# Gated block with a sliding, dilated attention: low halves of weights written by accumulating transfers, and tiles moved to multiples of 256 bytes

## The chip, the cores and the metric

The kernel runs on one core of one Trainium2 chip. The metric is device time in microseconds (us) of one execution, the median of several. Before the change it is 787.69 us, the median of 3 runs (787.12 to 788.05).

A core has a matrix engine (TensorE, PE in the profile; its weight loads stand apart as PEld), three engines that work element by element (VectorE or DVE, ScalarE or ACT, GpSimd or POOL), SyncE (SP), which issues transfers, and 16 DMA engines that move data between the main memory and SBUF, the core's memory of 128 partitions. A matmul has a stationary operand, which a weight load brings into the array, and a moving operand, which is streamed through it; both come from SBUF. Sums come out in PSUM.

## The reference

One block of 2048 tokens, 640 wide, in float32. With `xn` the layer norm of `x`:

```
qkv  = xn @ wqkv                      # 640 x 1920, 32 heads of 20
s    = attention(q, k, v) @ wo        # each token sees itself and 7 others, 2 apart
g    = silu(((xn @ w_gate) * (xn @ w_up)) @ w_down)    # inner width 1536
out  = x + s * g
```

## The kernel before, in words

**Two halves for every operand.** TensorE reads its operands as `float32r`, a rounded form of float32. To keep the precision, each operand is split in two: `hi`, the value rounded to `float32r`, and `lo`, the rest. A product is then three: hi by hi, hi by lo, lo by hi (`ALL3`, line 88; `mm3`, line 90, runs through the inner dimension once for each pair). Lines 83 to 86 make the halves of a weight: ScalarE copies `raw` to `hi`, which rounds, and then the engine that the caller names subtracts; for weights that is GpSimd, in all calls of this part.

**What runs on TensorE.** `qkv` (line 286) makes q, k and v for one of 12 units (6 groups of heads by 2 halves of the tokens): per tile of 128 tokens 15 matmuls, with the tokens `xT` stationary and `wqh` or `wql` moving, 300 columns (groups of 5 heads) or 360 (groups of 6). `gate_up` (line 387) makes one piece (f, ch), 128 columns of gate and of up for 512 tokens: 15 matmuls of 512 columns for each, with the weights `wf` stationary and `xT` moving. f runs from 0 to 11 and ch from 0 to 3. `out_proj` multiplies by `wo` (line 477) and `product` by `w_down` (line 596, with 7 products in place of 8); both have 320 columns.

**The order is written out by hand**, one engine's queue after the other's in program order. After a start with f = 0 and 1, units and pieces alternate: a unit of 8 tiles, then 3 or 4 pieces. In piece (f, 0) SyncE loads the raw weights of f + 1 (`load_wf`); in piece (f, 1), between gate and up, they are split (`split_wf`, line 123). The next group's q, k, v weights are loaded in the third tile of an odd unit (`load_wq`) and split at its end (`split_wq`, line 109), since `wqh` and `wql` have one buffer each, which this unit reads. VectorE works on the attention of earlier units in small steps between the products `hs` of gate and up (`advance`, line 371).

**Where tiles lie.** Tiles stand in a partition one behind the other, in the order in which their tags first appear, each rounded up to 32 bytes. In the built program the tags `t`, `wraw`, `xc` (which holds `xT` and later most of `w_down`), `o` and `ident` start 128 bytes past a multiple of 256; `wqh` starts 32 past one and `wql` 64; `q`, `kv`, `wf`, `mask`, `sel`, `gs`, `hs`, `ot`, `lg` and `e` start 96 past one. The rows that TensorE reads in `wf`, `xc` and the later weights are 512, 2048 or 1280 bytes apart, all multiples of 256, so every row stands as its tile does. The rows of `wqh` and `wql` are 1200 or 1440 bytes long and follow each other directly, so that each of the five stands differently: of `wqh` (300 columns) at 32, 208, 128, 48 and 224 past a multiple of 256, of `wql` at 64, 240, 160, 80 and 0.

Of the kernel before, what the change touches and what calls it, by code (L numbers as in the profile page):

```python
# [12 lines left out]
F32R = mybir.dt.float32r  # L13
AF = mybir.ActivationFunctionType
ALU = mybir.AluOpType
# [4 lines left out]
P = 128  # L20
# [6 lines left out]
KD, KF = D // P, F // P  # L27
# [23 lines left out]
def kernel(  # L51
# [11 lines left out]
    nc = tc.nc  # L63
# [11 lines left out]
    def st(shape, tag, bufs, dt=F32):  # L75
        cnt[0] += 1
        return sb.tile(shape, dt, tag=tag, bufs=bufs, name=f"{tag}_{cnt[0]}")

    def pt(shape, tag, bufs):
        cnt[0] += 1  # L80
        return ps.tile(shape, F32, tag=tag, bufs=bufs, name=f"{tag}_{cnt[0]}")

    def split(eng, raw, hi, lo):

        nc.scalar.activation(hi, raw, AF.Copy)  # L85
        eng.tensor_sub(lo, raw, hi.bitcast(F32))  # L86

    ALL3 = ((0, 0), (0, 1), (1, 0))

    def mm3(acc, pairs, parts=ALL3, first=True, last=True):  # L90

        pairs = list(pairs)
        runs = [(a[i], b[j]) for i, j in parts for a, b in pairs]
        for n, (a, b) in enumerate(runs):
            nc.tensor.matmul(acc, a, b, start=first and n == 0, stop=last and n == len(runs) - 1)  # L95


    wq_raw, wq = {}, {}
# [10 lines left out]
    def split_wq(g, eng, ks=(0, KD)):  # L109
        c3 = 3 * GROUPS[g] * DH  # L110
        if g not in wq:
            wq[g] = st([P, KD, c3], "wqh", 1, F32R), st([P, KD, c3], "wql", 1, F32R)
        for k0, k1, t in wq_raw[g]:
            if ks[0] <= k0 < ks[1]:
                split(eng, t, wq[g][0][:, k0:k1], wq[g][1][:, k0:k1])

    wf_raw, wf = {}, {}

# [3 lines left out]

    def split_wf(f, eng, cuts=(0, KD)):
        hi, lo = st([P, KD, 2, P], "wf", 4, F32R), st([P, KD, 2, P], "wf", 4, F32R)
        for k0, k1 in zip(cuts, cuts[1:]):
            split(eng, wf_raw[f][:, k0:k1], hi[:, k0:k1], lo[:, k0:k1])
        wf[f] = hi, lo


# [2 lines left out]
    def load_x(s, n, t, cuts=(0, D)):  # L132
        j = tile_column(s)
        for c0, c1 in zip(cuts, cuts[1:]):
            nc.sync.dma_start(t[:, :, c0:c1], (xbv if s < NE else xv)[:, j:j + DIL * (n - 1) + 1:DIL, c0:c1])  # L135
        for i in range(n):
            xt[s + i] = t[:, i, :]

    xa, xe = st([P, 3, D], "t", 2), st([P, 3, D], "t", 2)
    load_x(0, 1, xa[:, 0:1], (0, HALF, D))  # L140
    load_x(1, 1, xa[:, 1:2])
# [110 lines left out]
    def trans_odd(s):  # L252
# [7 lines left out]
        low_parts()  # L260
        halves.append(lambda: nc.vector.tensor_sub(lo, y, hi.bitcast(F32)))


    UN = [(g, r) for g in range(len(GROUPS)) for r in range(DIL)]
    q_t, kv_t, kv_buf, kv_zero = {}, {}, {}, {}
# [17 lines left out]

    ALL_RUNS = [(a, b, k) for a, b in ALL3 for k in range(KD)]

# [141 lines left out]
    def gate_up_first(f, ch):  # L427

        pp = [pt([P, CH], "g", 2), pt([P, CH], "u", 2)]
        for parts, first in ((ALL3[:2], True), (ALL3[2:], False)):  # L430
            for n in range(2):
# [6 lines left out]
    def load_wo(ks):  # L438
        t = st([P, 2, D], "wraw", 3)
        for n, k in enumerate(ks):  # L440
            nc.sync.dma_start(t[:, n, :], wo[:, k, :])
            wo_raw[k] = t[:, n, :]
        return t
# [192 lines left out]
    norm(0, 1)  # L636
    mv1 = moments(1, 1)
    split_wq(0, nc.gpsimd, (0, 2))
    trans(0)
    split_wq(0, nc.gpsimd, (2, 3))  # L640
    norm(1, 1, mv1)
    split_wq(0, nc.gpsimd, (3, KD))
    load_x(12, 1, xa[:, 0:1])
    begin_unit(0, False)
# [4 lines left out]
    moments(3, 1, mv2[:, 1:2])  # L649
    load_x(13, 1, xa[:, 1:2])  # L650
    split_wf(0, nc.gpsimd, range(KD + 1))
    norm(2, 2, mv2)
    qkv(0, 1)
    split_wf(1, nc.gpsimd, range(KD + 1))
    zero_front(0)
    part0 = gate_up_first(0, 0)
# [52 lines left out]
    gate_up(1, 2)  # L709
    gate_up(0, 3)  # L710
    split_wf(2, nc.gpsimd)
    gate_up(1, 3)

# [35 lines left out]
    for ch in range(NCH):  # L749
        gate_up(f0, ch)  # L750
        if ch == 0:
# [3 lines left out]
            t = load_wo((4,))  # L755
# [112 lines left out]
```

## Time and profile before

| | |
|---|---|
| median of 3 runs | 787.69 us (787.12 to 788.05) |
| the profiled execution | span 786.0 us from the first to the last instruction |
| mean granted TensorE clock | 0.999 |
| TensorE busy | 778.0 us, 4454 matmuls |
| weight loads busy | 708.9 us, beside the matmuls |
| VectorE, ScalarE, GpSimd busy | 659.3, 234.2, 147.9 us |
| read from and written to main memory | 54.53 MB, 28.31 MB |
| DMA engines, mean busy share of queue 1 | 38.2% |

The profile was taken in an execution of its own, so its span, 786.0 us, stands 1.7 us below the median of the timed runs. A row of a group has the line, the engine, the operation, the output and the inputs by tile name, the shape, the count, then the busy time and the mean of one in ns, and last the idle time of the engine in front of them with what ended it. In the chain of waits each row has a start, a duration and what the time was spent on; it is followed back from the last instruction. A row of the timeline has a start, the time to the end of the last of its instructions, the engine, and the instructions. A row of a table by stage has the stretch and its length, then for each engine the busy time and the count of instructions, the granted clock, the DMA share and GB/s.

### The profile page before, as it was taken

How to read it: one execution, taken by the hardware profiler on the slowest of the kernel's cores; microseconds unless marked ns; L12 is line 12 of the kernel's file. 1: busy time of each engine (PE TensorE's matmuls, PEld its weight loads, DVE VectorE, ACT ScalarE, POOL GpSimd, SP SyncE). 2: the span in 40 equal slices, each digit the busy share in tenths (PEclk: the TensorE clock that was granted, in tenths of full speed). 3: DMA queues.
4: the chain of work that ended last, by engine and by line, in shares of the span. 5: the costliest groups of instructions: out<-in, count | busy, mean ns of one | idle time of the engine just before them, and what ended most of it. 6: DMA issues, size and time to landing. Idle time of an engine off the chain costs nothing.

```text
span 786.0 us, 11222 instructions
## 1 busy us (share of the span) xinstructions
PE 778.0 (99%) x4454; PEld 708.9 (90%) x4454; DVE 659.3 (84%) x660; ACT 234.2 (30%) x536; POOL 147.9 (19%) x110
## 2 busy tenths in 40 slices
PE   8999999999999999999999999999999999999997
PEld 6889898888898898899898989888899999999997
DVE  6889899999999979996999999992177667777775
ACT  5334211121112111311221202012366564444442
POOL 5301211022013200410231000112467600000000
PEclk9999999999999999999999999999999999999999
DMA  8172122141132321404033131332797574555534
GB/s 321 67 230 75 42 61 72 48 123 48 50 83 89 95 71 61 117 28 112 28 105 86 58 86 58 107 103 66 160 274 209 170 270 131 206 200 188 182 101 135
DMA packets 81661, 92.68 MB, mean 118 GB/s; under 512 B 23032, under 2 KB 63304, under 8 KB 81480
## 3 DMA queue, kind: packets, MB, share of 16 engines
q1 hardware_dynamic: 81608, 91.96, 38.2%
q8 instruction: 35, 0.57, 0.3%
q14 instruction: 18, 0.15, 0.1%
HBM read 54.53 MB, written 28.31 MB: 105 GB/s over the span
## 4 chain that ended last, share of the span: by engine, by line
PE 97%; DMA 2%; ACT 1%; DVE 0%; SPq 0%; POOL 0%; issue 0%
PE q L295 26%; PE u L95 21%; PE g L95 21%; PE q L606 11%; PE q L95 9%; PE u L606 5%; PE g L606 3%; DMA wraw<-in_wgu 1%; DMA wraw<-in_wqkv 1%; PE q L229 0%; ACT wf L85 0%; SPq L135 0%; ACT wqh L85 0%; ACT xc L230 0%; POOL wql L86 0%; PE q L249 0%
## 5 line engine op out<-in xcount | busy, mean ns | idle before, releaser
L95 PE MATMUL u<-xc,wf 128*128 128x512 f32 (+1 forms) x735 | 176.2, 390 | 0.0
L95 PE MATMUL g<-xc,wf 128*128 128x512 f32 (+1 forms) x735 | 176.1, 390 | 0.0
L95 PEld LDWEIGHTS u<-xc,wf 128*128 128x128 f32 x735 | 135.7, 187 | 32.2
L95 PEld LDWEIGHTS g<-xc,wf 128*128 128x128 f32 x735 | 135.3, 187 | 31.0
L295 PE MATMUL q<-wqh,xc 128*128 128x300 f32 (+1 forms) x960 | 159.8, 309 | 2.1 <-DVE xc L231 1.2
L295 PEld LDWEIGHTS q<-wqh,xc 128*128 128x128 f32 x960 | 146.0, 188 | 4.3 <-DVE xc L231 1.5
L329 DVE TENSOR_TENSOR t<-q,kv 128x1600 f32<-128x1600 f32 (+1 forms) x48 | 97.9, 2040 | 10.1 <-DMA kv<-kv 10.1
L350 DVE TENSOR_TENSOR t<-e,kv 128x1600 f32<-128x1600 f32 (+1 forms) x48 | 97.5, 2051 | 1.1
L86 POOL TENSOR_TENSOR wf<-wraw,wf 128x256 fp32r<-128x256 f32 (+2 forms) x22 | 48.8, 2232 | 248.1 <-ACT wf L85 248.1
L332 DVE TENSOR_REDUCE lg<-t 128x80 f32<-128x1600 f32 (+1 forms) x48 | 92.6, 1930 | 1.2
L397 ACT ACTIVATE gs<-g 128x512 f32<-128x512 f32 x48 | 28.7, 598 | 205.9 <-PE g L95 197.2
L295 PE MATMUL q<-wql,xc 128*128 128x300 f32 (+1 forms) x480 | 86.3, 309 | 0.0
L358 DVE TENSOR_TENSOR t<-t,t 128x1600 f32<-128x1600 f32 (+1 forms) x36 | 80.2, 2228 | 1.1
L295 PEld LDWEIGHTS q<-wql,xc 128*128 128x128 f32 x480 | 74.4, 188 | 0.0
L297 ACT ACTIVATE kv<-q 128x200 f32<-128x200 f32 (+1 forms) x96 | 33.4, 348 | 129.4 <-PE q L295 129.4
L606 PE MATMUL q<-xc,wf 128*128 128x320 f32 x432 | 67.3, 309 | 0.0
L606 PEld LDWEIGHTS q<-xc,wf 128*128 128x128 f32 x432 | 64.3, 188 | 0.0
L86 POOL TENSOR_TENSOR wql<-wraw,wqh 128x300 fp32r<-128x300 f32 (+4 forms) x15 | 34.0, 2292 | 142.7 <-ACT wqh L85 142.7
L95 PE MATMUL q<-wf,wf 128*128 128x320 f32 x156 | 35.7, 310 | 0.0
L408 DVE TENSOR_TENSOR hs<-u,gs 128x512 f32<-128x512 f32 x39 | 26.6, 683 | 0.6 <-issue 0.6
L95 PEld LDWEIGHTS q<-wf,wf 128*128 128x128 f32 x156 | 26.1, 188 | 0.0
L86 DVE TENSOR_TENSOR wf<-ot,wf 128x640 fp32r<-128x640 f32 x13 | 15.5, 1190 | 11.9 <-ACT wf L85 11.9
(161 smaller groups left out, 888.9 us busy)
## 6 DMA issues: line engine op xcount, KB each, us to landing
h_scr<-hs SPq DMA_DIRECT2D x48, 256.0 KB, 2.3
wraw<-in_wgu SPq DMA_DIRECT2D x12, 640.0 KB, 4.9
t<-h_scr SPq DMA_DIRECT2D x8, 768.0 KB, 7.8
hs<-s_scr SPq DMA_DIRECT2D x16, 320.0 KB, 4.0
gs<-in_x SPq DMA_DIRECT2D x16, 320.0 KB, 4.4
wraw<-h_scr SPq DMA_DIRECT2D x12, 384.0 KB, 5.9
out<-q SPq DMA_DIRECT2D x14, 320.0 KB, 3.7
wraw<-in_wd SPq DMA_DIRECT2D x12, 320.0 KB, 4.8
```

The source lines that it names most:

```text
L86: eng.tensor_sub(lo, raw, hi.bitcast(F32))
L95: nc.tensor.matmul(acc, a, b, start=first and n == 0, stop=last and n == len(runs) - 1)
L295: nc.tensor.matmul(p, xT[(r * NE + i) // TPC][a][:, k, t0:t0 + P], wq[g][b][:, k], start=n == 0, stop=n == len(runs) - 1, skip_group_check ...
L297: nc.scalar.activation(kv_t[u][:, :, W - 1 + i, :], p[:, c:].rearrange("p (a c) -> p a c", a=2), AF.Copy)
L329: nc.vector.tensor_mul(t, q.rearrange("p i c -> p (i c)").unsqueeze(1).to_broadcast([P, 2, NE * c]), places(0, j))
L332: nc.vector.tensor_reduce(out=lg[:, :, j:j + 2].rearrange("p n a -> p a n"), in_=heads(t), op=ALU.add, axis=AX.X)
L350: nc.vector.tensor_mul(heads(t), pw, heads(places(1, j)))
L358: nc.vector.tensor_add(acc, acc, t)
L397: nc.scalar.activation(gs, pp[0], AF.Copy)
L408: nc.vector.tensor_mul(hs, pp[1], gs)
L606: nc.tensor.matmul(p, y[:, i, k], wd_t[name][k][:, l], start=new and r == 0, stop=r == len(runs) - 1, skip_group_check=True)
```

## The change

It has two parts.

**The low halves of most weights.** For the gate and up weights of f = 2 to 11 and the q, k, v weights of groups 1 to 5, GpSimd's subtraction goes. ScalarE now writes `lo` as well, as the copy of `raw` times -1, and then GpSimd issues a transfer that reads the same weights from main memory again and adds them onto `lo`, which gives raw - hi. The weights of f = 0 and 1 and of group 0 are split as before, as are those of the later stages.

**Addresses.** Two tiles that nothing uses are put in, `skip` (128 bytes) ahead of all others and `gap` (96 bytes) behind the small tiles, and the rows of `wqh` and `wql` are padded to a multiple of 64 elements, 1280 and 1536 bytes. With that every tile that TensorE reads as `float32r` starts at a multiple of 256 bytes, and each of its rows does.

```
+    def split_dma(raw, src, hi, lo):
+
+        nc.scalar.activation(hi, raw, AF.Copy)
+        nc.scalar.activation(lo, raw, AF.Copy, scale=-1.0)
+        nc.gpsimd.dma_start(lo, src, accum_op=ALU.add)
...
-            wq[g] = st([P, KD, c3], "wqh", 1, F32R), st([P, KD, c3], "wql", 1, F32R)
+            cp = -(-c3 // 64) * 64
+            wq[g] = [st([P, KD, cp], tag, 1, F32R)[:, :, :c3] for tag in ("wqh", "wql")]
         for k0, k1, t in wq_raw[g]:
             if ks[0] <= k0 < ks[1]:
-                split(eng, t, wq[g][0][:, k0:k1], wq[g][1][:, k0:k1])
+                if g:
+                    split_dma(t, wqkv[g][:, k0:k1, :], wq[g][0][:, k0:k1], wq[g][1][:, k0:k1])
+                else:
+                    split(eng, t, wq[g][0][:, k0:k1], wq[g][1][:, k0:k1])
...
-        for k0, k1 in zip(cuts, cuts[1:]):
-            split(eng, wf_raw[f][:, k0:k1], hi[:, k0:k1], lo[:, k0:k1])
+        if f > 1:
+            split_dma(wf_raw[f], wgu[f], hi, lo)
+        else:
+            for k0, k1 in zip(cuts, cuts[1:]):
+                split(eng, wf_raw[f][:, k0:k1], hi[:, k0:k1], lo[:, k0:k1])
...
+    st([P, 32], "skip", 1)
     xa, xe = st([P, 3, D], "t", 2), st([P, 3, D], "t", 2)
...
+    st([P, 24], "gap", 1)
```

On ScalarE the change shows at the end of the fourth unit, where the weights of group 2 are split, and in the second piece after it, where those of f = 4 are. A name's number counts the tiles and differs between the programs. Before:

```order
L297 ACTIVATE kv_757<-q_1617 128x2x100
L298 ACTIVATE q_1465<-q_1617 128x100
L85 ACTIVATE wqh_1638<-wraw_1508 128x900
L85 ACTIVATE wqh_1638<-wraw_1510 128x600
L397 ACTIVATE gs_1663<-g_1646 128x512
L397 ACTIVATE gs_1700<-g_1683 128x512
L85 ACTIVATE wf_1702<-wraw_1644 128x1280
```

The same place on ScalarE after the change, where line 90 writes the high half and line 91 the negative into the low one:

```order
L313 ACTIVATE kv_759<-q_1623 128x2x100
L314 ACTIVATE q_1471<-q_1623 128x100
L90 ACTIVATE wqh_1644<-wraw_1514 128x3x300
L91 ACTIVATE wql_1645<-wraw_1514 128x3x300
L90 ACTIVATE wqh_1644<-wraw_1516 128x2x300
L91 ACTIVATE wql_1645<-wraw_1516 128x2x300
L413 ACTIVATE gs_1671<-g_1654 128x512
L413 ACTIVATE gs_1708<-g_1691 128x512
L90 ACTIVATE wf_1710<-wraw_1652 128x1280
L91 ACTIVATE wf_1711<-wraw_1652 128x1280
```

Each copy has a second one behind it, ahead of the copies `gs` out of PSUM. GpSimd's queue at the same place, from f = 3 to group 3, before:

```order
L86 TENSOR_TENSOR wf_1352<-wraw_1288,wf_1351 128x1280
L86 TENSOR_TENSOR wql_1639<-wraw_1508,wqh_1638 128x900
L86 TENSOR_TENSOR wql_1639<-wraw_1510,wqh_1638 128x600
L86 TENSOR_TENSOR wf_1703<-wraw_1644,wf_1702 128x1280
L86 TENSOR_TENSOR wf_2053<-wraw_1988,wf_2052 128x1280
```

And after it:

```order
L92 DMA wf_1357<-in_wgu 128x1280
L92 DMA wql_1645<-in_wqkv 128x3x300
L92 DMA wql_1645<-in_wqkv 128x2x300
L92 DMA wf_1711<-in_wgu 128x1280
L92 DMA wf_2062<-in_wgu 128x1280
```

Every subtraction has become one transfer in the same place of the queue, 20 in all. The queues of TensorE, VectorE and SyncE hold the same instructions in the same order as before.

## The prediction

> **What bounds the kernel now.** I read the page first: busy times, then the chain of waits by engine.
>
> ```profile
> PE 778.0 (99%) x4454; PEld 708.9 (90%) x4454; DVE 659.3 (84%) x660; ACT 234.2 (30%) x536; POOL 147.9 (19%) x110
> ...
> PE 97%; DMA 2%; ACT 1%; DVE 0%; SPq 0%; POOL 0%; issue 0%
> ```
>
> The chain is 97% TensorE. The table by stage (length, then busy time of each engine, clock, DMA share, GB/s) shows where it is not:
>
> ```profile
> 0.00:20.25 20.25, 16.48 (x89) 12.54 (x89) 13.07 (x42) 10.65 (x31) 10.90 (x20) 1.00 0.90 324
> 20.25:121.45 101.20, 101.20 (x599) 91.50 (x600) 90.79 (x145) 29.85 (x79) 18.93 (x20) 1.00 0.29 91
> 121.45:563.36 441.91, 441.91 (x2282) 386.75 (x2282) 394.29 (x273) 86.87 (x224) 75.25 (x28) 1.00 0.28 79
> 563.36:781.75 218.39, 218.37 (x1489) 218.11 (x1487) 160.17 (x200) 106.37 (x202) 42.79 (x43) 1.00 0.61 191
> 781.75:786.00 4.25, 0.00 (x0) 0.00 (x0) 0.98 (x2) 0.44 (x1) 0.00 (x0) 0.88 0.22 79
> ```
>
> The start takes 20.25 us, then TensorE is busy without a hole for 101.20 + 441.91 + 218.39 = 761.5 us at a granted clock of 1.00, and 4.25 us of output follow. So only three things can move the time: the start, the pace of one matmul behind another, and a new wait of TensorE. The waits of all TensorE's instructions are these, all within the start:
>
> ```profile
> PE q L157 <- POOL ident masks.py:199: 1.4, 1, 1.4
> PE q L295 <- DVE xc L231: 1.2, 1, 1.2
> PE q L295 <- ACT xc L230: 0.9, 2, 0.6
> PE q L229 <- issue: 0.3, 1, 0.3
> ```
>
> GpSimd releases TensorE once, with the identity matrix, which the change leaves alone.
>
> **GpSimd's subtractions go: 0.** The large ones are
>
> ```profile
> L86 POOL TENSOR_TENSOR wf<-wraw,wf 128x1280 fp32r<-128x1280 f32 x10 | 38.6, 3864 | 245.1 <-ACT wf L85 245.1
> L86 POOL TENSOR_TENSOR wql<-wraw,wqh 128x600 fp32r<-128x600 f32 x3 | 9.2, 3065 | 0.0
> L86 POOL TENSOR_TENSOR wql<-wraw,wqh 128x900 fp32r<-128x900 f32 x3 | 8.0, 2653 | 59.2 <-ACT wqh L85 59.2
> L86 POOL TENSOR_TENSOR wql<-wraw,wqh 128x1080 fp32r<-128x1080 f32 x2 | 6.6, 3310 | 77.7 <-ACT wqh L85 77.7
> L86 POOL TENSOR_TENSOR wql<-wraw,wqh 128x720 fp32r<-128x720 f32 x2 | 6.1, 3074 | 0.0
> ```
>
> 38.6 + 9.2 + 8.0 + 6.6 + 6.1 = 68.5 us, all in the two stages in which TensorE has no hole, so nothing waits for them. VectorE may run faster with GpSimd silent; it too releases nothing there.
>
> **ScalarE copies twice: 0.** A second copy lasts about as long as the first, 1.27 us for `wf` (row below) and 1.55 us for a group's two parts. That is 10 x 1.27 + 5 x about 1.6 = some 21 us on an engine that is busy 87 of 442 us in that stage. In its queue stands behind it the next `gs` copy. At the end of a unit:
>
> ```profile
> 165.97 0.34 ACT L297 ACTIVATE kv<-q 128x200 f32<-128x200 f32 x1 [1.58 <-PE q L295]
> ...
> 166.33 1.55 ACT L85 ACTIVATE wqh<-wraw 128x900 fp32r<-128x900 f32 x2
> ...
> 169.52 0.60 ACT L397 ACTIVATE gs<-g 128x512 f32<-128x512 f32 x1 [1.64 <-PE g L95]
> ```
>
> The copies would now end near 166.33 + 2 x 1.6 = 169.5, just where `gs` starts. If they cover it by half a microsecond, TensorE doesn't see it: g has two buffers in PSUM, and the one that `gs` frees is needed a whole piece later. Without that second buffer it would be 0.5 us in each of five places.
>
> **The accumulating transfers: 0, if they land in 16 us.** No row of before shows one. The nearest are the plain loads of the same bytes:
>
> ```profile
> wraw<-in_wgu SPq DMA_DIRECT2D x12, 640.0 KB, 4.9
> ...
> wraw<-in_wqkv SPq DMA_DIRECT2D x3, 450.0 KB, 3.9
> ```
>
> The time to beat comes from the timeline. The tightest hand-over is that of f = 10, whose copy starts in piece (9, 1) and whose first use follows two pieces on; `mm3` needs `lo` from the eleventh of the 15 matmuls on. The tightest of the q, k, v weights have three pieces in between:
>
> ```profile
> 490.45 1.27 ACT L85 ACTIVATE wf<-wraw 128x1280 fp32r<-128x1280 f32 x1
> ...
> 507.20 3.66 PE L95 MATMUL g<-xc,wf 128*128 128x512 f32 x15
> ...
> 187.45 0.43 PE L295 MATMUL q<-wql,xc 128*128 128x300 f32 x2
> ```
>
> For f = 10 `lo` is written by 490.45 + 2 x 1.27 = 492.99 and needed at 507.20 + 10 x 0.233 = 509.53: 16.5 us for the issue on GpSimd, the transfer and its landing. For group 2 it is 187.45 - (166.33 + 1.55 + 1.66) = 17.9 us. I bound a transfer by the plain load, 4.9 us, and by 20 us, four times that, since it also reads and rewrites SBUF. I take the lower half, some 5 to 10 us, as nearest to the row of the same size: cost 0. It adds 10 x 640 KB and five groups, about 10.7 MB on the 54.53 that are read, in stages with a DMA share of 0.28. On GpSimd's queue the transfer waits for ScalarE as the subtraction did, and nothing but the next one of its kind stands behind.
>
> **The addresses: -0.2 us.** What matters is the pace. From the chain of waits:
>
> ```profile
> 149.45 16.48 PE q L295 x120
> 165.93 3.50 PE g L95 x15
> 344.05 19.84 PE q L295 x120
> 563.36 70.60 PE q L95 x480
> 633.96 2.64 PE q L606 x18
> ...
> 779.10 2.65 PE q L606 x18
> 781.75 0.02 issue
> ```
>
> Per column of the moving operand this is 16.48 / (120 x 300) = 0.4578 ns for q, k, v with 300 columns, 19.84 / (120 x 360) = 0.4593 with 360, 3.50 / (15 x 512) = 0.4557 for gate and up, 70.60 / (480 x 320) = 0.4596 for the output projection, and (781.75 - 633.96) / (1008 x 320) = 0.4582 for the products. These five have five different mixes of addresses and differ by 0.9%. The five rows of `wql` include one at a multiple of 256 bytes and those of `wqh` none, with the same stationary tiles:
>
> ```profile
> 107.55 0.85 PE L295 MATMUL q<-wql,xc 128*128 128x300 f32 x5
> 108.24 1.53 PE L295 MATMUL q<-wqh,xc 128*128 128x300 f32 x10
> 109.61 0.85 PE L295 MATMUL q<-wql,xc 128*128 128x300 f32 x5
> ```
>
> Five of `wql` take 108.24 - 107.55 = 0.69 us, ten of `wqh` 109.61 - 108.24 = 1.37 us: 138 and 137 ns. One aligned row among five shows no gain, so where a moving row starts does not set the pace. What before never shows is a stationary tile at a multiple of 256, or both operands there. Bounds: all at the best pace, 0.4557, gives 288,000 columns x 0.0021 + 172,800 x 0.0036 + 153,600 x 0.0039 + 322,560 x 0.0025 = 2.6 us less; all at the worst, 0.4596, gives 737,280 x 0.0039 + 288,000 x 0.0018 + 172,800 x 0.0003 + 322,560 x 0.0014 = 3.9 us more. I take the one step that has a near row: the output projection, whose tiles stand in four different ways, at the pace of the products, which have the same 320 columns: 153,600 x 0.0014 = 0.2 us less.
>
> [...]
>
> **The sum**: 786.0 - 0.2 for the span; with the 1.7 us between span and median, 787.5.
>
> **The rivals.**
> - *Pace evens out* (faster). If misplaced rows are what sets the five paces apart, all go to the best: 787.7 - 2.6 = 785.1 us. For it: the two that mix addresses most, 0.4593 and 0.4596, are the slowest. Against: products from `xc` and `kv`, 128 and 96 past a multiple, share one pace, 2.64 and 2.65 us per 18.
> - *The stall is due to the stationary tiles* (much faster). All 4454 weight loads start off a multiple of 256. Each row of PEld has 187 to 188 ns for a load, beside 233 for a 512-column matmul; if matmuls fell to that, gate and up would lose 1410 x 45 ns = 63 us, and half of it, as the middle of 0 and 63, gives 756. [...]
>
> ```profile
> L95 PEld LDWEIGHTS u<-xc,wf 128*128 128x128 f32 x735 | 135.7, 187 | 32.2
> ```
>
> - *Both streams on the same lines* (slower). With every operand at 0 of 256, load and stream may meet more often than the mixed addresses of before let them: the worst pace for all, 787.7 + 3.9 = 791.6. It decides as soon as gate and up, 338 of the 761.5 us, go from 233.3 to over 234.5 ns.
> - *Low halves come late* (slower). GpSimd builds these transfers while VectorE is busy 394 of 442 us. If one takes 20 us from copy to landing, f = 10 costs 3.5 us and three groups at 2.1 us each 6.3: 797.5. It decides from 16.5 us. Against: the plain load's 4.9. The Trainium skill (SBUF — State Buffer, Who interferes with whom) says that a transfer issued by GpSimd is held up while VectorE is in a two-port mode; this trace has no such transfer, and the instructions that fill VectorE there are TENSOR_TENSOR and TENSOR_REDUCE, which that section counts out.
> - *The change doesn't do what it says*: GpSimd's work leaves, but no engine waited for it. That is part of the forecast.
>
> **How the numbers follow.** A measurement of this kernel can tell about 0.2%, 1.6 us. Forecast, 787.5: 0.46. Pace evens out, 785.1: 0.20. Stationary stall, 756: 0.12. Same lines, 791.6: 0.14. Late halves, 797.5: 0.08. Faster 0.20 + 0.12 = 0.32, within 0.2% 0.46, slower 0.22. The range leaves out the stationary stall and the late halves, 0.20, and takes in the rest: down to 787.7 - 2 x 2.6 - 0.6 = 781.9, the gain doubled because before has no pair with both operands at 256, less the spread of the runs (787.69 - 787.12), and up to 791.6 + 0.4. Alone the forecast has 786.1 to 789.2.
>
> **What would show it.** TensorE without a wait after the start, 3.50 us per 15 matmuls of 512 columns, 16.48 and 19.84 us for 120 of q, k, v, and 70.4 us for the output projection. Transfers `wql<-in_wqkv` and `wf<-in_wgu` that land within 10 us of their issue. ScalarE some 21 us busier, GpSimd some 68 us less. The forecast is wrong if the rows of gate and up are shorter or longer than 3.48 to 3.52 us, or if TensorE waits for a low half.

## The result, and the profile after

The kernel became faster: 775.69 us, the median of 4 runs (775.42 to 775.79), against 787.87 us (787.12 to 789.47) for the kernel before in the same session. The ratio is 0.9843, with a 95% interval of 0.9829 to 0.9857. The profiled execution has a span of 773.8 us, 12.2 us less than before, and a mean granted clock of 1.000. The forecast was 787.5 us with a range of 781.9 to 792.0, so the time lies below the range.

The page of the kernel after, its busy times, its traffic, its chain of waits by engine, and two rows of its transfers (size, median us from issue to landing):

```profile
PE 765.1 (99%) x4454; PEld 705.9 (91%) x4454; DVE 631.5 (82%) x660; ACT 254.4 (33%) x556; POOL 101.3 (13%) x110
...
HBM read 65.23 MB, written 28.31 MB: 121 GB/s over the span
...
PE 97%; DMA 2%; ACT 0%; POOL 0%; DVE 0%; SPq 0%; issue 0%; POOLq 0%
...
wraw<-in_wgu SPq DMA_DIRECT2D x12, 640.0 KB, 5.6
wf<-in_wgu POOLq DMA_DIRECT2D x10, 640.0 KB, 6.1
```

The chain is still 97% TensorE, with the same 4454 matmuls. So TensorE does the same work in less time, and the table by stage (stretch and length, then busy time and count of PE, PEld, DVE, ACT, POOL, the clock, the DMA share and GB/s) shows in which stage:

```profile
0.00:20.18 20.18, 16.05 (x88) 12.48 (x88) 12.85 (x42) 10.69 (x31) 10.92 (x20) 1.00 0.90 323
...
121.50:550.96 429.46, 429.46 (x2277) 382.92 (x2276) 366.23 (x270) 104.19 (x239) 33.66 (x28) 1.00 0.41 103
550.96:769.21 218.25, 218.23 (x1488) 217.97 (x1487) 160.09 (x200) 106.15 (x202) 43.56 (x43) 1.00 0.59 191
769.21:773.80 4.59, 0.00 (x0) 0.00 (x0) 0.99 (x2) 0.44 (x1) 0.00 (x0) 0.94 0.19 71
```

The start (20.18 us, 20.25 before), the output at the end (4.59, 4.25 before) and the last stage of matmuls (218.25, 218.39 before) are as they were. TensorE's stretch without a hole went from 761.5 to 769.21 - 20.18 = 749.0 us, and nearly all of that is in the part with q, k, v, gate and up. The chain of waits of the kernel after (start, duration, what) gives the pace:

```profile
60.16 16.40 PE q L311 x120
76.56 3.40 PE g L101 x15
...
338.16 19.20 PE q L311 x120
...
550.96 70.39 PE q L101 x480
621.35 2.64 PE q L622 x18
```

Against the rows of before, 15 matmuls of 512 columns take 3.40 us for 3.50 (226.7 ns each for 233.3), 120 of 360 columns 19.20 for 19.84, 120 of 300 columns 16.40 for 16.48, the output projection 70.39 for 70.60, and the products the same 2.64. With the 94 groups of gate and up that have 512 columns (2 x 705 matmuls; the first four groups have 256), 4 units of 360 and 8 of 300 columns, that is 94 x 0.10 + 4 x 0.64 + 8 x 0.08 + 0.21 = 12.8 us by these rounded rows, where the stretch lost 12.5. **The whole gain is the pace of matmuls, about three quarters of it that of gate and up.** The waits of TensorE's instructions are still those of the start alone (from the engine and line, the one waited for, the time in total, how often, the longest):

```profile
PE q L311 <- DVE xc L245: 1.6, 1, 1.6
PE q L171 <- POOL ident masks.py:199: 1.4, 1, 1.4
PE q L311 <- ACT xc L244: 0.9, 2, 0.6
```

The change has two parts, transfers and addresses, and the pace alone doesn't say whether GpSimd's silence, the transfers or the places of the operands set it. The theories were these. *Place*: the pace depends on where the operands lie, and of that there are three forms (the moving one must stand at a multiple of 256 bytes, the stationary one must, or the two must stand alike). *Traffic*: with GpSimd no longer reading and writing SBUF, TensorE's reads are faster. *Both parts needed*: one makes room that the other uses.

### The profile page after: what moved, and what is told of

Same layout as the page of the kernel before. It is cut to its first block, busy times and chain, and to the rows that moved or that the text cites. A ratio compares the mean times of both kernels' runs of the same rounds, so it can differ in the third digit from the quotient of the medians.

```text
span 773.8 us, 11232 instructions
## 1 busy us (share of the span) xinstructions
PE 765.1 (99%) x4454; PEld 705.9 (91%) x4454; DVE 631.5 (82%) x660; ACT 254.4 (33%) x556; POOL 101.3 (13%) x110
## 4 chain that ended last, share of the span: by engine, by line
PE 97%; DMA 2%; ACT 0%; POOL 0%; DVE 0%; SPq 0%; issue 0%; POOLq 0%
PE q L311 26%; PE u L101 21%; PE g L101 21%; PE q L622 11%; PE q L101 9%; PE u L622 5%; PE g L622 3%; DMA wraw<-in_wgu 1%; DMA wraw<-in_wqkv 0%; PE q L243 0%; POOL wql L86 0%; ACT wf L85 0%; SPq L148 0%; PE q L263 0%; DVE xc L245 0%
## 5 line engine op out<-in xcount | busy, mean ns | idle before, releaser
L101 PE MATMUL u<-xc,wf 128*128 128x512 f32 (+1 forms) x735 | 171.8, 385 | 0.0
L101 PE MATMUL g<-xc,wf 128*128 128x512 f32 (+1 forms) x735 | 171.7, 385 | 0.0
L311 PE MATMUL q<-wqh,xc 128*128 128x300 f32 (+1 forms) x960 | 157.6, 307 | 2.5 <-DVE xc L245 1.6
L311 PEld LDWEIGHTS q<-wqh,xc 128*128 128x128 f32 x960 | 144.1, 188 | 4.4 <-DVE xc L245 1.8
L345 DVE TENSOR_TENSOR t<-q,kv 128x1600 f32<-128x1600 f32 (+1 forms) x48 | 92.5, 1928 | 16.3 <-DMA kv<-kv 16.3
L366 DVE TENSOR_TENSOR t<-e,kv 128x1600 f32<-128x1600 f32 (+1 forms) x48 | 91.9, 1934 | 1.1
L374 DVE TENSOR_TENSOR t<-t,t 128x1600 f32<-128x1600 f32 (+1 forms) x36 | 69.7, 1935 | 1.1
L92 POOL DMA_DIRECT2D wf<-in_wgu x10 | 8.8, 879 | 270.2 <-ACT wf L91 181.9
L92 POOL DMA_DIRECT2D wql<-in_wqkv x10 | 12.7, 1322 | 147.8 <-ACT wql L91 147.7
L86 DVE TENSOR_TENSOR wf<-ot,wf 128x640 fp32r<-128x640 f32 x13 | 14.2, 1096 | 12.7 <-ACT wf L85 12.7
```

The source lines that it names most:

```text
L92: nc.gpsimd.dma_start(lo, src, accum_op=ALU.add)
L311: nc.tensor.matmul(p, xT[(r * NE + i) // TPC][a][:, k, t0:t0 + P], wq[g][b][:, k], start=n == 0, stop=n == len(runs) - 1, skip_group_check ...
L345: nc.vector.tensor_mul(t, q.rearrange("p i c -> p (i c)").unsqueeze(1).to_broadcast([P, 2, NE * c]), places(0, j))
L366: nc.vector.tensor_mul(heads(t), pw, heads(places(1, j)))
L374: nc.vector.tensor_add(acc, acc, t)
```

## The experiments

Each diff is against the kernel after, unless it says otherwise. Ratios are to the kernel before, on the same chip.

### One part alone: the transfers

```diff
-            cp = -(-c3 // 64) * 64
-            wq[g] = [st([P, KD, cp], tag, 1, F32R)[:, :, :c3] for tag in ("wqh", "wql")]
+            wq[g] = [st([P, KD, c3], tag, 1, F32R)[:, :, :c3] for tag in ("wqh", "wql")]
...
-    st([P, 32], "skip", 1)
...
-    st([P, 24], "gap", 1)
```

> The kernel before with the accumulating transfers alone; every tile stands where it did. Theory A (the addresses make the whole gain): gate and up stay at 3.50 us per 15 matmuls of 512 columns, 120 matmuls of 300 columns take 16.48 us and of 360 columns 19.84 us, no wait of TensorE, ratio to before 0.998 to 1.002. Theory B (the silent GpSimd makes part of it): rows of gate and up below 3.45 us in the stages where GpSimd no longer subtracts, ratio 0.985 to 0.997. Theory C (the transfers cost something that the addresses paid for): ratio over 1.002, with TensorE waiting for a low half.

It took 787.87 us (median of 10), ratio 1.0003 (0.9993 to 1.0012). The chain of waits of this kernel has the pace of before:

```profile
104.24 16.48 PE q L308 x120
120.72 3.50 PE g L101 x15
...
343.11 19.84 PE q L308 x120
```

So the transfers by themselves are worth nothing, and *traffic* falls: GpSimd's twenty subtractions are gone here too, and the pace didn't move.

### The other part alone: the addresses

```diff
-                if g:
+                if False:
...
-        if f > 1:
+        if False:
```

> The addresses of the changed kernel, with all low halves by GpSimd as before. Theory A: 3.40 us per 15 matmuls of 512 columns, 19.20 us for 120 of 360 columns, 16.40 us for 120 of 300, ratio to before 0.983 to 0.986, the changed kernel's own. Theory B: less of a gain, a ratio of 0.987 to 0.998. Theory C: more, below 0.982.

It took 790.69 us (median of 4), ratio 1.0043 (1.0026 to 1.006): **slower than before**, which none of the three expected ratios allowed for, though gate and up run at the new pace wherever nothing holds them (one row of its chain of waits stands here):

```profile
76.44 3.40 PE g L101 x15
```

The waits of TensorE in this kernel show what took the gain back:

```profile
PE u L101 <- DVE hs L424: 8.1, 6, 2.2
PE q L311 <- ACT q L314: 1.7, 2, 1.1
```

Neither row is there in before or in after. The timeline of one such place in this kernel (start, time to the end of the last, engine, what, and in brackets the wait):

```profile
374.50 2.16 DVE L345 TENSOR_TENSOR t<-q,kv 128x1920 f32<-128x1920 f32 x1 [6.21 <-DMA kv<-kv]
...
377.26 2.96 POOL L86 TENSOR_TENSOR wf<-wraw,wf 128x1280 fp32r<-128x1280 f32 x1 [40.72 <-ACT wf L85]
377.36 3.56 PE L101 MATMUL g<-xc,wf 128*128 128x512 f32 x15
378.77 3.46 DVE L345 TENSOR_TENSOR t<-q,kv 128x1920 f32<-128x1920 f32 x1
...
382.89 5.30 PE L101 MATMUL u<-xc,wf 128*128 128x512 f32 x15 [1.96 <-DVE hs L424]
```

While GpSimd subtracts, from 377.26 to 380.22, VectorE's product `t` takes 3.46 us where the same form takes 2.16 a moment earlier. Behind it `hs`, which empties a PSUM buffer of `u`, comes late, and the next matmuls of `u` wait for that buffer, 1.96 us. They then take 5.30 us and not 3.56, and a table over this place shows why:

```profile
382.90:384.30 1.40, 1.40 (x6) 1.18 (x7) 1.40 (x1) 0.60 (x1) 0.00 (x0) 1.00 0.40 123
384.30:387.00 2.70, 2.70 (x9) 2.07 (x8) 2.67 (x3) 0.00 (x0) 0.00 (x0) 0.52 0.12 36
```

The granted clock falls to 0.52 behind this hole, so here the matmuls after it ran at about half pace as well. It is the only place of this stage where that is so. Behind the longest hole, 2.17 us before the matmuls of `u` at 341.03, the clock stays at 1.00:

```profile
341.02:344.50 3.48, 3.47 (x15) 2.90 (x16) 3.45 (x3) 0.60 (x1) 0.00 (x0) 1.00 0.25 75
```

What makes the clock fall behind the one and not behind the other isn't shown. The same stage as in the table of after, 121.50 to the output projection, has this row here:

```profile
121.50:565.78 444.28, 434.50 (x2274) 384.47 (x2273) 403.00 (x272) 85.29 (x222) 70.91 (x28) 1.00 0.27 78
```

That is 444.28 - 429.46 = 14.8 us more than after, of which 444.28 - 434.50 = 9.8 us are holes; the other 5.0 are longer matmul times. The one stretch at half clock, some 3.4 us long, makes about 1.7 us of these by an estimate; the rest is open. VectorE is busy for 403.00 us of the stage, where after has 366.23, and the chain of waits, which before has 0% on VectorE, here spends 9.9 + 9.2 + 7.7 + 4.6 + 2.5 = 33.9% of the span on its products, sums and `hs`. The faster TensorE makes VectorE the bound, unless GpSimd leaves it alone: the parts alone are worth 0.0% and +0.4%, and together -1.6%.

### GpSimd's reads put back, and writes in their place

Behind each transfer GpSimd gets work that nobody uses: a subtraction into a dummy tile (two inputs from SBUF), or three memsets of it (writes alone).

```diff
         nc.gpsimd.dma_start(lo, src, accum_op=ALU.add)
+        nc.gpsimd.tensor_sub(d, raw, hi.bitcast(F32))
```

```diff
         nc.gpsimd.dma_start(lo, src, accum_op=ALU.add)
+        for _ in range(3):
+            nc.gpsimd.memset(d, 0.0)
```

> The changed kernel with the old subtraction put back on GpSimd beside the transfers, into a tile that nothing reads (line 100): the result is as before, GpSimd is as busy as it was. Theory V (with aligned operands VectorE is the next to be late, since its two-input instructions stand still while GpSimd reads SBUF): VectorE's products of 1600 elements go from 1.82 to 2.0-2.3 us, TensorE waits for hs, time 787 to 792 us. Rival T (the transfers themselves shorten something else): 775 to 777 us.

> The changed kernel with three fills of the same unused tile on GpSimd in place of that subtraction: GpSimd is busy for about as long but reads nothing. Theory V with reads alone as the cause: VectorE stays at 1.82 us per 1600 elements, 775 to 777 us. Rival (any GpSimd work beside VectorE, or its instructions' mere number, slows it): 2.0 us and more, 785 us and up.

With the reads it took 784.85 us (median of 6), ratio 0.9967 (0.9953 to 0.998); with the writes 775.54 (2 runs), ratio 0.9847 (0.9819 to 0.9876), the same as after. VectorE's groups by form tell it (behind the first bar stand the busy time in us and the mean of one in ns). Before, two instructions with two inputs and between them one with one input:

```profile
L329 DVE TENSOR_TENSOR t<-q,kv 128x1600 f32<-128x1600 f32 x32 | 63.3, 1977 | 4.3 <-DMA kv<-kv 4.3
L332 DVE TENSOR_REDUCE lg<-t 128x80 f32<-128x1600 f32 x32 | 58.2, 1819 | 0.8
L358 DVE TENSOR_TENSOR t<-t,t 128x1600 f32<-128x1600 f32 x24 | 52.1, 2170 | 0.7
```

After, the two with two inputs:

```profile
L345 DVE TENSOR_TENSOR t<-q,kv 128x1600 f32<-128x1600 f32 x32 | 58.1, 1817 | 7.9 <-DMA kv<-kv 7.9
L374 DVE TENSOR_TENSOR t<-t,t 128x1600 f32<-128x1600 f32 x24 | 43.8, 1824 | 0.7
```

With GpSimd's reads put back, all three again:

```profile
L353 DVE TENSOR_TENSOR t<-q,kv 128x1600 f32<-128x1600 f32 x32 | 64.4, 2012 | 4.4 <-DMA kv<-kv 4.4
L356 DVE TENSOR_REDUCE lg<-t 128x80 f32<-128x1600 f32 x32 | 58.2, 1819 | 0.8
L382 DVE TENSOR_TENSOR t<-t,t 128x1600 f32<-128x1600 f32 x24 | 54.6, 2273 | 0.7
```

And with writes in their place, the first:

```profile
L351 DVE TENSOR_TENSOR t<-q,kv 128x1600 f32<-128x1600 f32 x32 | 58.1, 1817 | 7.9 <-DMA kv<-kv 7.9
```

An instruction with two inputs from SBUF takes 1.82 us undisturbed and 2.0 to 2.3 on average when GpSimd's subtractions run somewhere beside it; the reduction, with one input, has 1819 ns before as with the reads; memsets disturb nothing, though GpSimd is busier with them (160.0 us) than with the subtractions (156.5). With the reads TensorE waits for `hs` again, 5.2 us in total, where the addresses alone have 8.1. The Trainium skill (SBUF — State Buffer, Who interferes with whom) says that a VectorE instruction with two SBUF inputs contends with a GpSimd instruction that reads SBUF, and not with one that only writes it. These four groups of rows agree.

The size fell short of the 787 to 792 us expected with the reads: 784.85 - 775.69 = 9.2 us given back, where the addresses alone gave back 15.0 (790.69 - 775.69) at nearly the same busy time of VectorE (667.6 and 668.5 us). In the one the results of the subtractions are used and in the other not, and they stand elsewhere in GpSimd's queue; which of the two makes the difference wasn't tried.

### Which operand must stand where

Three shifts of the same tiles, with the transfers of after: the moving one at 0 and the stationary one 96 bytes past a multiple of 256 (for gate and up), the moving one at 128 and the stationary one at 0, and both at 128.

```diff
-    st([P, 24], "gap", 1)
+    st([P, 48], "gap", 1)
```

```diff
-    st([P, 32], "skip", 1)
...
-    st([P, 24], "gap", 1)
+    st([P, 56], "gap", 1)
```

```diff
-    st([P, 32], "skip", 1)
```

> The changed kernel with the gap 96 bytes wider: the tiles in front of it stand at multiples of 256 bytes, wf, wqh, wql and the later ones 96 past one. In gate and up the moving operand is at 0 and the stationary one at 96; in q, k, v it is the other way round. If the moving operand alone sets the pace: gate and up 3.40 us per 15, q, k, v with 360 columns back at about 19.84 us per 120. If the stationary one alone does: gate and up 3.50, 360 columns at 19.20. If both must stand at a multiple of 256: 3.50 and 19.84.

> The changed kernel without skip and with the gap 128 bytes wider: t, xc and the others in front of the gap stand 128 past a multiple of 256 bytes, wf, wqh, wql and the later ones at one. In gate and up the moving operand is at 128 and the stationary one at 0; in q, k, v it is the other way round. If the moving operand alone sets the pace with a step of 256 bytes: gate and up 3.50 us per 15, 360 columns 19.20 us per 120. If the stationary one alone does: 3.40 and 19.84. If both must: 3.50 and 19.84. If 128 bytes are enough for either: 3.40 and 19.20.

> The changed kernel without skip: every operand of TensorE stands 128 past a multiple of 256 bytes, rows of wqh and wql too. If an operand only has to start at a multiple of 128, or both must only stand alike: 3.40 us per 15 matmuls of 512 columns, 19.20 us per 120 of 360, 775.7 us. If it takes a multiple of 256: 3.45 to 3.52 us, 19.8 to 20.0 us, 785 to 790 us.

The first took 791.88 us and the second 789.93 (one run each), the third 775.40 (2 runs), ratio 0.9846 (0.9817 to 0.9874). From the chain of waits of the first, a group of up and 120 of q, k, v with 300 columns (there the tokens are the stationary operand, so the places are exchanged):

```profile
87.67 3.52 PE u L101 x15
...
105.24 16.79 PE q L311 x120
```

The same of the second:

```profile
88.70 3.48 PE u L101 x15
...
106.14 16.67 PE q L310 x120
```

And of the third:

```profile
83.05 3.40 PE g L101 x15
...
103.45 16.40 PE q L310 x120
```

One operand at a multiple of 256 bytes, whichever it is, leaves gate and up within 0.02 us of the 3.50 of before, and q, k, v are even slower than the 16.48 of before. Both at 128, where not one of them is at a multiple of 256, have the full pace of after. **So what counts is that the two operands stand alike modulo 256 bytes**; the multiple itself isn't needed.

### The pace by itself

Two kernels with matmuls alone, which leave the block's computation out: eight stationary and eight moving tiles at 0, 32, ... 224 past a multiple of 256 in all 64 pairs, and one stationary tile with the moving one ahead of it by steps from 4 bytes on. Nothing else runs beside them.

```
    for s in LETTERS:
        for m in LETTERS:
            group(s, m, 512)
...
    for n in (512, 320, 300, 360):
        for j, d in enumerate(AHEAD):
            group(LETTERS[j % 8], d, n)
```

> A kernel of its own that leaves out the whole computation and only runs matmuls: 30 of 512 columns for each of 8 starts of the stationary operand (sta to sth: 0, 32, ... 224 bytes past a multiple of 256) by 8 of the moving one (mva to mvh, into PSUM tiles pa to ph), then 30 each of 256, 300, 320, 360, 384, 448 and 480 columns for the starts 0/0, 96/128, 96/96 and 0/96. No other engine works beside them. If both operands must stand at a multiple of 256: 6.80 us per 30 for sta with mva and about 7.0 for all others. If a multiple of 128 is enough: 6.80 also for sta/mve, ste/mva, ste/mve. If they must only stand alike: 6.80 on the whole diagonal. If the difference of before and after came from other engines' traffic: the same figure everywhere.

> Leaves out the whole computation and only runs matmuls with nothing beside them: the stationary operand at a multiple of 256 bytes, the moving one ahead of such a multiple by -64, -48, -32, -16, -8, -4, 0, 4, 8, 16, 24, 32, 48, 64, 80, 96, 112, 128, 256, 512, 768, 1024, 2048 and 4096 bytes, 30 matmuls each, first with 512 columns, then 320, 300, 360. If the place of one operand against the other modulo 256 bytes sets the pace: with 512 columns 6.80 us per 30 at 0, 256, 512 and all larger ones, 6.87 at 64, 7.00 elsewhere. If it is modulo something larger (512 or more): 6.80 at 0 alone and not at all of 256 to 4096. If what remains above one cycle per column comes from a meeting of the two streams: some offset below 6.75.

The chain of the first has one row for 30 matmuls of 512 columns. These four have the stationary tile at 32, and the moving one (`pa` to `pd`) at 0, 32, 64 and 96:

```profile
77.15 6.99 PE pa L45 x30
84.14 6.83 PE pb L45 x30
90.97 7.00 PE pc L45 x30
97.97 6.87 PE pd L45 x30
```

The fast one is the pair that stands alike, 6.83; a moving tile 64 bytes ahead has 6.87, all others about 7.0. The first set begins with a row of 8.75 us, the first matmuls of that kernel; in the seven sets of eight behind it the dip moves with the stationary tile: 6.80 to 6.83 where the two stand alike, 6.86 or 6.87 at 64 ahead, 6.97 to 7.03 elsewhere. These are the sizes seen in the kernels: 7.00 / 30 = 233 ns as before, and 6.80 / 30 = 226.7 as after. With no other engine at work, *traffic* is out here too.

In the second kernel's chain the moving tile is first 16 bytes behind the stationary one's place, then 8 and 4 behind, alike, and 4 ahead:

```profile
50.85 6.80 PE pd L45 x30
57.65 7.04 PE pe L45 x30
64.69 6.92 PE pf L45 x30
71.61 6.80 PE pg L45 x30
78.41 7.12 PE ph L45 x30
```

Not a smooth dip: 16 behind and alike are fast, what lies between is not. At 256 ahead it is 6.85, and from 512 to 4096 ahead all have 6.80, so larger distances hardly matter. No place has less than 6.80. How much the place is worth depends on the columns: 320 columns have 4.40 per 30 (146.7 ns) nearly everywhere, which fits that the products didn't move at all and the output projection hardly did; 300 have 4.10 to 4.20 per 30, but 4.02 at 80 ahead; 360 have 4.81 alike, 4.80 at 112 ahead and 4.92 to 5.06 elsewhere. There is a limit to this reading: with 360 columns a distance of 256 to 4096, the same place modulo 256, had 4.93 to 4.94 per 30 and not 4.81. The first kernel shows it too: with 360 columns and both operands at 0 it has 4.93, and by the starts of the matmuls in its trace 4.81 with both at 96.

```profile
515.68 4.93 PE pa L45 x30
```

Nor does 300 alike carry over: alone it has 4.14 to 4.20 per 30, and in the block after, 16.40 / 4 = 4.10. So the place modulo 256 is not all of it, and what else is stays open; the pace of 512 columns, three quarters of the gain, is the same in both, 226.7 ns.

### Rows not padded, and other offsets

```diff
-            cp = -(-c3 // 64) * 64
-            wq[g] = [st([P, KD, cp], tag, 1, F32R)[:, :, :c3] for tag in ("wqh", "wql")]
+            wq[g] = [st([P, KD, c3], tag, 1, F32R)[:, :, :c3] for tag in ("wqh", "wql")]
...
-    st([P, 32], "skip", 1)
...
-    st([P, 24], "gap", 1)
+    st([P, 8], "gap", 1)
```

> The accumulating transfers as in the changed kernel, without skip and without padded rows, and the gap 32 bytes wide, so that wf, q, kv and the later tiles stand 128 past a multiple of 256 bytes, as xc does: only gate and up, the products and part of the output projection have their two operands alike, while the rows of wqh and wql stand as variously as before. If the place of the two operands against each other is the cause, stage by stage: 3.40 us per 15 matmuls of 512 columns, 16.48 and 19.84 us per 120 of 300 and 360, and 787.7 - 94 x (3.50 - 3.40) = 778.3 us. If an address of its own counts (a multiple of 256 for the moving or the stationary operand): 3.50 and 787.7.

This leaves `wf` and `xT` alike (both at 128) and the rows of q, k, v mixed as in before. It took 780.46 us (2 runs), ratio 0.9909 (0.989 to 0.9929), with 3.40 us for gate and up, but 16.62 and 19.84 for q, k, v. So with the transfers in place the `gap` alone, without padding, carries 787.56 - 780.46 = 7.1 of the 12.2 us, and the padded and aligned rows the rest. It fell some 2 us short of what was expected: 8 x (16.62 - 16.48) = 1.1 us of that is the units with 300 columns, slower than before with another mixture of places, and 0.7 is gate and up, whose groups on the chain of waits fell from 332.5 to 323.8 us in sum, by 8.7 and not 94 x 0.10 = 9.4.

Last, the two best offsets of the second kernel of matmuls were tried: rows of 300 columns 80 bytes on, and the stationary tile of the products 4 bytes on (320 columns had 4.31 per 30 with the moving one 4 behind).

```diff
+            ahead = 20 if cp == 320 else 0
...
-        hT[m] = st([P, 2, KH, P], "wf", 4, F32R)
+        y = st([P, 2 * KH * P + 64], "wf", 4, F32R)[:, 1:1 + 2 * KH * P]
```

> The changed kernel with two more moves taken from the fine table: rows of wqh and wql with 300 columns start 80 bytes past a multiple of 256, and hT, the stationary operand of the products, 4 bytes past one. If the pace found with one matmul kind alone holds in the kernel: 4.00 us per 30 matmuls of 300 columns, so 16.0 us per 120 in place of 16.40, and 2.58 us per 18 products in place of 2.64; that is 8 x 0.40 + 56 x 0.06 = 6.6 us less, 769 us. If those two figures hang on how the streams happened to meet and not on the start alone: 775 to 777, with single rows faster or slower.

It took 773.69 us (median of 4), ratio 0.9824 (0.9807 to 0.984). From its chain of waits:

```profile
103.27 16.03 PE q L315 x120
```

The 16.03 us per 120 are the 4.02 per 30 found with matmuls alone, and over 8 units 8 x 0.37 = 3.0 us. The products stayed at 2.64 us per 18: the gain at 4 bytes did not carry over to them, and why is open. So the 769 us expected were missed. This is the fastest version seen, some 2 us below the kernel after (span 771.4 for 773.8), though the intervals of the two ratios overlap.

## Why the prediction was wrong, step by step

- **What can move the time**: "the start, the pace of one matmul behind another, and a new wait of TensorE". Right. It was the pace, and with the addresses alone a new wait as well.
- **GpSimd's subtractions, 0**: right for the pace of before, where taking them away gave 1.0003. The cover was named as TensorE without a hole, and the speed-up of VectorE was seen, but "it too releases nothing there" held only as long as the pace did. VectorE was busy 394.29 of the 441.91 us of that stage; with TensorE 12 us faster, the disturbed VectorE is late, and the addresses alone cost 3 us.
- **ScalarE copies twice, 0**: right. It is 254.4 - 234.2 = 20.2 us busier, for 21 forecast, and nothing waits for it. GpSimd's own drop was overstated: 147.9 - 101.3 = 46.6 us for 68, since the 20 transfers keep it busy while it issues them, 8.8 + 12.7 us by these rows of its groups after:

```profile
L92 POOL DMA_DIRECT2D wql<-in_wqkv x10 | 12.7, 1322 | 147.8 <-ACT wql L91 147.7
L92 POOL DMA_DIRECT2D wf<-in_wgu x10 | 8.8, 879 | 270.2 <-ACT wf L91 181.9 <-PE u L101 64.8 <-ACT e L357 22.0
```

- **Accumulating transfers in time, 0**: right. Those of `wf` land in 6.1 us and those of `wql` in 5.6 to 8.8, by the medians (5 to 10 forecast, 16.5 to beat), and they add the 10.7 MB that were counted.
- **The addresses, -0.2 us**: this is the step that failed. The sentence was "One aligned row among five shows no gain, so where a moving row starts does not set the pace". The place of that one row was taken against the memory, not against its stationary tile, which stood at 128, so that the aligned row was an unlike pair. The row that did stand alike with its tokens was another one, the third of `wqh`, at 128. And the size was one that hardly feels the place: with every pair alike, 120 matmuls of 300 columns went only from 16.48 to 16.40 us. The bounds failed with it: "all at the best pace" took the best of five mixtures, and gate and up, the best of them, was itself an unlike pair (96 against 128), 6.7 ns above what an alike pair has. "What before never shows is a stationary tile at a multiple of 256, or both operands there" was written down, and then bounded by rows that don't show it either. The term, put at -0.2 us, measured -12.5 us.
- **Rivals.** *Pace evens out* had the right sign and a fifth of the size, 2.6 us. *The stall is due to the stationary tiles* was wrong in its mechanism: a stationary tile at 0 alone gains nothing for q, k, v, and weight loads still have 188 ns. *Both streams on the same lines* had the right variable, the place of one against the other, and the wrong sign: gate and up went to 226.7 ns, not over 234.5. *Low halves come late* didn't happen. The forecast named its own test, rows of gate and up below 3.48 us, and they are at 3.40.

Why unlike places cost a matmul 6.7 ns isn't shown by these runs; only that it hangs on the places of TensorE's own two operands against each other (no other engine ran beside the matmuls of the two kernels of their own), and that for 512 columns 512 to 4096 bytes more between them cost nothing.

## What to carry to other kernels

When TensorE runs without a hole, compare the pace of its rows with that of the same matmuls by themselves, over a few places of the two operands against each other: a gap of 3% spread over all matmuls shows in no list of waits. Try what is found there in the block, since not every figure carried over. A step that bounds an unseen arrangement by rows that don't contain it has no bound; measure it, or give it a wide one. And when the bounding engine gets faster, look at once at the next one: here GpSimd's reads of SBUF beside VectorE's two-input instructions took back 9 to 15 us of a gain of 12, and the gain was there because the same change also took these reads away.

## What the runs showed of the hardware that was not expected

- A matmul of 512 columns with a weight load each takes 226.7 to 227.7 ns when both operands stand alike modulo 256 bytes, 229 when the moving one is 64 ahead, and 232 to 234 otherwise, over places 32 bytes apart; in finer steps 16 bytes behind is as fast as alike and 4 ahead the slowest, 7.12 / 30 = 237 ns. With 320 columns it is 146.7 nearly everywhere, with 300 the best is 80 ahead (16.03 / 120 = 133.6 ns in the block), and with 256 columns the matmuls alone took 3.59 us per 30 alike and 3.50 with 32 between the two. There is no one best place for all sizes.
- A hole of 1.96 us in TensorE's stream was followed, 1.4 us after it resumed, by 2.7 us at a granted clock of 0.52; behind one of 2.17 us in the same run the clock stayed at 1.00.
- An accumulating transfer of 640 KB that GpSimd issues from main memory onto SBUF lands 6.1 us after its issue, beside 5.6 for a plain load of the same bytes, and keeps GpSimd for 0.88 us.
